# Loading one block's inputs early, spreading its query projection over the other block's attention, and moving a final projection

## The chip, the cores and the metric

One core of a Trainium2 chip runs the whole program. The metric is the device time of one execution in microseconds. The engines are TensorE (PE: matmuls; PEld: its weight loads), VectorE (DVE), ScalarE (ACT), GpSimd (POOL) and SyncE (SP), which here issues every transfer.

## The reference

Two independent attention blocks on inputs of 2048 tokens and 640 channels, with 32 heads of 20 channels, in bfloat16. Their results stand side by side in the output, A in columns 0 to 639 and B in columns 640 to 1279.

```python
# A: four segments of 512 tokens; inside a segment causal attention, beside it a
#    memory M, z of all earlier segments
logits = einsum('bhqd,bhkd->bhqk', qs, ks) * scale + mask
a_dot = einsum('bhqk,bhkd->bhqd', softmax(logits), vs)
pq = phi(qs)                       # phi(t) = t + 1 if t > 0 else exp(t)
a_mem = einsum('bhld,bhde->bhle', pq, M) / (einsum('bhld,bhd->bhl', pq, z) + 1e-6)
o = g * a_mem + (1 - g) * a_dot    # g = sigmoid(beta), per head
M = M + einsum('bhld,bhle->bhde', phi(ks), vs);  z = z + sum(phi(ks))
out_A = concat(o) @ A_wo
# B: causal attention in a window of 256 tokens
q, k, v = split(B_x @ B_wqkv)
scores = where(0 <= i - j < 256, q @ k.T * scale, -1e9)
out_B = (softmax(scores) @ v) @ B_wo
```

## The kernel before

Tokens come in 16 tiles of 128, heads in 8 groups of four; a head of 20 channels is padded to 32 partitions. The program is written stage after stage with tile pools; a scheduler puts each engine's instructions in one fixed order, mostly that of the text, and an engine runs its own in that order. A tile of a pool that takes the memory of a released pool waits for the last users of that memory.

The stages in order of time:

1. **B's projections.** `load_w` fetches wo_A and wo_B, `load_xT` fetches B's input transposed (xT_B, five transposing transfers), then comes the weight wallB. `proj_qk_compact_to_dram` makes the keys (kcB) and the queries (qcB), 20 steps of five 512-column matmuls each, and stores each result in one transfer to DRAM (kcdB, qcdB). `proj_v` makes the values in 16 tiles, five matmuls of 512 columns and five of 128 each; VectorE evicts them into vaug_B. PSUM has two buffers for either kind.
2. **A's keys and values.** The pool p2 opens when stage 1's pool closes. Into it go xT_A (five transposing transfers), wraw_k, wv_A and wraw_q. VectorE scales wv_A with a row made from beta, and copies wraw_k and wraw_q into zeroed padded weights (wk_pad, wq_pad; GpSimd zeroes them). `proj_qk_padded_to_dram` makes the padded keys in 32 steps of five 512-column matmuls, eight steps to a 1 MB store of stp0 or stp1 to kdA; `proj_v` makes the values, two tiles to a store of vstA0 or vstA1 to vdA.
3. **B's attention** (`attention_B`): for each head group g, 16 iterations kt over key tiles. An iteration makes scores of four heads (L298, up to 384 query columns), ScalarE turns them into probabilities pt (L305, two instructions, at most 768 elements wide), VectorE masks the diagonal (L307), GpSimd the far edge (L313). Every second iteration multiplies pt with the values (L341, 16 matmuls of 128 or 256 columns), and `normalize_block` transposes and divides (L226 to L244) into o_tok_B. The two PSUM buffers psS hold the scores. The keys and queries of a group are fetched into kg0, kg1, qg0 and qg1 in turn, zero-filled once from zt. At the end of each iteration `next(aux_gen)` traces one step of A's query projection: 32 steps like those of the keys (PSUM ppa, evicted into stp0 and stp1), and after every eighth a store to qdA.
4. **B's final projection** (`final_projection`): for each token tile five transposes, an eviction, five matmuls of 512 columns and five of 128, an eviction, and the store.
5. **A's segments** (`segment_A`): four times, for 512 tokens: k_s, v_s and q_s are fetched from kdA, vdA and qdA; for each head group the feature maps (ek, eq, pkt, pq), scores (L429), ScalarE's exponentials (L437), GpSimd's mask (L443), the value matmuls (L462), the memory products (L406, L473); at the segment's end the final projection of its own four tiles.

Of the kernel before, what the change touches and what calls it, by code (L numbers as in the profile page):

```python
# [8 lines left out]
ALU = mybir.AluOpType  # L9
# [3 lines left out]
P = 128  # L13
# [9 lines left out]
class _K:  # L23
# [250 lines left out]
    def attention_B(self, wk, psum, qcd, kcd, vaug, o_tok, aux_gen=None):  # L274
# [8 lines left out]
        for g in range(G):  # L283
# [6 lines left out]
            for kt in range(T):  # L290
# [62 lines left out]
                if aux_gen is not None:  # L353
                    next(aux_gen, None)
# [140 lines left out]
    def run(self, A_x, A_wq, A_wk, A_wv, A_wo, A_beta, B_x, B_wqkv, B_wo, out2d):  # L495
# [8 lines left out]
        with tc.tile_pool(name="pers", bufs=1) as pers:  # L504
            wo_A = self.load_w(pers, "wo_A", A_wo)
            wo_B = self.load_w(pers, "wo_B", B_wo)
            with tc.tile_pool(name="ob", bufs=1) as pob:
                o_tok_B = pob.tile([P, T, D], BF16, name="o_tok_B")
                vaug_B = self.make_vaug_sbuf(pob, "vaug_B")
                pp1 = self.ctx_psum1 = tc.alloc_tile_pool(name="ps1pool", bufs=1,  # L510
                                                          space=bass.MemoryType.PSUM)
                self.build_consts(A_beta, pp1)

                def get_ps_1():
                    return pp1.tile([P, 512], F32, name="pps1", bufs=2)

                def get_ps2_1():
                    return pp1.tile([P, 2, 512], F32, name="pps2", bufs=2)
                with tc.tile_pool(name="p1b", bufs=1) as p1:
                    xT_B = self.load_xT(p1, B_x[0], "xT_B")  # L520
                    wall = self.load_w(p1, "wallB", B_wqkv)
                    qcB = p1.tile([P, MC, S], BF16, name="qcB")
                    kcB = p1.tile([P, MC, S], BF16, name="kcB")

                    def vsink_b(tt, flat):
                        nc.vector.tensor_copy(
                            out=vaug_B[:, tt, :, 0:DH],
                            in_=flat[:, 0:D].rearrange("p (h e) -> p h e", e=DH))
                    for _ in self.proj_qk_compact_to_dram(wall[:, :, D:2 * D], xT_B,
                                                          kcB, kcdB, get_ps_1):  # L530
                        pass
                    for _ in self.proj_qk_compact_to_dram(wall[:, :, 0:D], xT_B, qcB,
                                                          qcdB, get_ps_1):
                        pass
                    for _ in self.proj_v(wall[:, :, 2 * D:3 * D], xT_B, get_ps2_1,
                                         vsink_b):
                        pass
                p2 = tc.alloc_tile_pool(name="p2", bufs=1)
# [4 lines left out]
                nc.vector.tensor_tensor(  # L543
                    out=wv_A[:], in0=wv_A[:],
                    in1=self.omh640[:].unsqueeze(1).to_broadcast([P, KT, D]),
                    op=ALU.mult)
                wk_pad = self.pad_weight(p2, "wk_padA", wraw_k[:])
                wq_pad = self.pad_weight(p2, "wq_padA", wraw_q[:])
                stps = [p2.tile([P, G, 512], BF16, name="stp0"),
                        p2.tile([P, G, 512], BF16, name="stp1")]  # L550
                vsts = [self.make_vst(p2, "vstA0", 2), self.make_vst(p2, "vstA1", 2)]

                def vsink_a(tt, flat):
# [12 lines left out]
                with tc.tile_pool(name="ps2pool", bufs=1, space=bass.MemoryType.PSUM) as pp2:  # L566
# [11 lines left out]
                    for _ in agen:  # L578
                        pass
# [76 lines left out]
```

## Time and profile before

| | us |
|---|---|
| median of four runs | 838.94 (837.62 to 842.25) |
| the profiled execution | 837.62 |
| its span | 835.9 |
| TensorE matmuls busy | 716.3 (86% of the span) |
| VectorE busy | 416.9 (50%) |
| ScalarE busy | 374.5 (45%) |
| GpSimd busy | 242.5 (29%) |

The busy shares are averages over stages that have different limits. The page's slices give the TensorE clock that was granted in each fortieth of the span; in the rows below it stands behind the busy times, and there 1.00 is 2.4 GHz and 0.50 is 1.2 GHz. The same instruction counts as busy for longer at the lower clock, so a busy share has to be read beside the clock.

### The profile page before, as it was taken

The page shows a single profiled execution, that of the slowest core. Times are in us where ns is not written, and L with a number is a line of the kernel's source. Part 1 is how long each engine was busy: PE and PEld are TensorE (multiplying, and loading weights), DVE is VectorE, ACT ScalarE, POOL GpSimd, SP SyncE. Part 2 cuts the span into 40 slices and gives each one's busy share as a digit, 9 for nine tenths or more (in the row PEclk, how much of TensorE's full clock was granted, in tenths as well). Part 3 has the DMA queues.
Part 4 walks back from the last instruction along what each step waited for, and adds up shares of the span by engine and source line. Part 5 has one row for each costly group of instructions (what it writes and reads, how often), then busy time and mean ns, then how long its engine had stood idle before and what let it go on. Part 6 is the DMA issues. An engine that isn't in the chain of part 4 may idle for free.

```text
span 835.9 us, 12231 instructions
## 1 busy us (share of the span) xinstructions
PE 716.3 (86%) x4768; PEld 308.3 (37%) x4768; DVE 416.9 (50%) x1013; ACT 374.5 (45%) x498; POOL 242.5 (29%) x498
## 2 busy tenths in 40 slices
PE   2799559999999999999998828887998898988996
PEld 1345324444444333333334413334333433342333
DVE  5366356566666544444444533235455745463343
ACT  0000000045658767666672017663666366526651
POOL 9000410023334424333341004331433134313431
PEclk9999869999999755555556975557555755565557
DMA  9434553421212100101000263005000500000000
GB/s 224 135 136 148 111 164 122 180 102 51 83 66 68 32 27 7 32 1 33 1 1 16 79 224 110 1 1 183 1 2 1 182 1 1 1 24 9 1 0 32
DMA packets 54028, 54.26 MB, mean 65 GB/s; under 512 B 22802, under 2 KB 46482, under 8 KB 53970
## 3 DMA queue, kind: packets, MB, share of 16 engines
q1 hardware_dynamic: 53970, 53.49, 20.4%
q8 instruction: 37, 0.61, 0.3%
q14 instruction: 21, 0.17, 0.1%
HBM read 24.38 MB, written 23.07 MB: 57 GB/s over the span
## 4 chain that ended last, share of the span: by engine, by line
PE 60%; DVE 10%; ACT 9%; POOL 7%; issue 6%; DMA 4%; SPq 4%; DVEq 0%; ACTq 0%
PE psO L341 11%; PE ps L462 9%; POOL pt L443 7%; PE psS L298 6%; ACT pt L437 6%; PE pps L147 5%; DVE oc L226 5%; PE pps L181 4%; PE ps L429 4%; PE pps L197 4%; SPq L119 3%; PE ppa L181 3%; PE ps L262 3%; PE fps L262 2%; ACT pt L305 2%
## 5 line engine op out<-in xcount | busy, mean ns | idle before, releaser
L305 ACT ACTIVATE pt<-psS 128x768 bf16<-128x768 f32 (+2 forms) x256 | 185.6, 770 | 253.8 <-PE psS L298 208.2
L437 ACT ACTIVATE pt<-ps 128x1024 bf16<-128x1024 f32 (+1 forms) x192 | 161.7, 881 | 96.2 <-PE ps L429 86.2
L443 POOL TENSOR_SCALAR_AFFINE_SELECT pt<-pt 128x256 bf16<-128x256 bf16 x256 | 105.8, 432 | 229.6 <-ACT pt L437 226.5
L313 POOL TENSOR_SCALAR_AFFINE_SELECT pt<-pt 128x256 bf16<-128x256 bf16 x224 | 103.7, 463 | 233.7 <-ACT pt L305 233.7
L462 PE MATMUL ps<-pt,v_s 128*32 128x128 bf16 (+3 forms) x512 | 117.4, 455 | 11.0 <-POOL pt L443 7.5
L341 PE MATMUL psO<-pt,vaug_B 128*32 128x256 bf16 (+1 forms) x960 | 126.0, 316 | 0.4
L298 PE MATMUL psS<-qg,kg 32*128 32x384 bf16 (+2 forms) x512 | 100.6, 414 | 6.6 <-ACT pt L305 5.3
L307 DVE TENSOR_TENSOR pt<-pt,cmask 128x256 bf16<-128x256 bf16 x256 | 79.8, 312 | 52.0 <-ACT pt L305 50.4
L429 PE MATMUL ps<-q_s,k_s 32*128 32x128 bf16 (+3 forms) x512 | 93.6, 433 | 11.8 <-ACT pt L437 7.8
L226 DVE CAST oc<-ps 128x512 bf16<-128x512 f32 x56 | 38.5, 688 | 95.2 <-PE ps L462 93.1
L341 PEld LDWEIGHTS <-vaug_B 128*32 128x32 bf16 x960 | 59.7, 110 | 68.9 <-issue 57.4
L462 PEld LDWEIGHTS <-v_s 128*32 128x32 bf16 x512 | 39.7, 119 | 75.6 <-issue 73.3
L226 DVE CAST oc<-psO 128x256 bf16<-128x256 f32 x64 | 27.1, 423 | 60.6 <-PE psO L341 60.5
L181 PE MATMUL pps<-xT_A,wk_padA 128*128 128x512 bf16 x160 | 36.8, 394 | 17.9 <-DVE wk_padA L133 17.9
L228 PEld LDWEIGHTS <-oc 128*128 128x128 bf16 x352 | 27.9, 120 | 61.3 <-DVE oc L226 60.8
L147 PE MATMUL pps<-xT_B,wallB 128*128 128x512 bf16 x200 | 45.1, 390 | 5.3 <-DMA wallB<-in_B_wqkv_dram 5.3
L379 ACT ACTIVATE ek<-k_s 128x512 bf16<-128x512 bf16 x24 | 14.9, 624 | 74.0 <-DMA k_s<-kdA 46.9
L429 PEld LDWEIGHTS <-k_s 32*128 32x128 bf16 x512 | 20.7, 100 | 73.5 <-issue 72.5
L181 PE MATMUL ppa<-xT_A,wq_padA 128*128 128x512 bf16 x160 | 44.7, 380 | 3.0 <-DVE stp L184 2.4
L298 PEld LDWEIGHTS <-kg 32*128 32x128 bf16 x512 | 25.0, 96 | 58.3 <-issue 50.5
L228 PE MATMUL ps<-ident,oc 128*128 128x128 bf16 x224 | 33.3, 302 | 14.4 <-DVE oc L226 14.4
L147 PEld LDWEIGHTS <-wallB 128*128 128x128 bf16 x200 | 19.9, 100 | 30.1 <-DMA wallB<-in_B_wqkv_dram 5.4
(97 smaller groups left out, 684.5 us busy)
## 6 DMA issues: line engine op xcount, KB each, us to landing
out_dram<-otile SPq DMA_DIRECT2D x32, 160.0 KB
kdA<-stp SPq DMA_DIRECT2D x4, 1024.0 KB
vdA<-vstA SPq DMA_DIRECT2D x8, 512.0 KB
qdA<-stp SPq DMA_DIRECT2D x4, 1024.0 KB
k_s<-kdA SPq DMA_DIRECT2D x4, 1024.0 KB
v_s<-vdA SPq DMA_DIRECT2D x4, 1024.0 KB
q_s<-qdA SPq DMA_DIRECT2D x4, 1024.0 KB
kcdB<-kcB SPq DMA_DIRECT2D x1, 2560.0 KB
```

Source lines behind the costliest of these rows:

```text
L147: nc.tensor.matmul(ps[:, 0:512], lhsT=w_ap[:, kt, m * P:(m + 1) * P], rhs=xT[:, kt, cs], start=(kt == 0), stop=(kt == KT - 1))
L181: nc.tensor.matmul(ps[:, 0:512], lhsT=wpad[:, kt, g * P:(g + 1) * P], rhs=xT[:, kt, cs], start=(kt == 0), stop=(kt == KT - 1))
L226: nc.vector.tensor_copy(out=oc[:, 0:ncols], in_=num_ps[:, 0:ncols])
L298: nc.tensor.matmul(pss[hp][:, i, 0:N], lhsT=kg[rows, kt * P:(kt + 1) * P], rhs=qg[rows, kt * P:kt * P + N], start=True, stop=True, tile_po ...
L305: nc.scalar.activation(out=pt[:, :, 0:N], in_=pss[hp][:, :, 0:N], func=ACT.Exp, scale=scale)
L307: nc.vector.tensor_tensor(out=pt[:, :, 0:P], in0=pt[:, :, 0:P], in1=self.cmask[:].unsqueeze(1).to_broadcast([P, 2, P]), op=ALU.mult)
L313: nc.gpsimd.affine_select(out=blk, in_=blk, pattern=[[0, 2], [-1, P]], compare_op=ALU.is_ge, fill=0.0, base=-1, channel_multiplier=1)
L341: nc.tensor.matmul(O[orows, oc0:oc0 + ncol], lhsT=vg[:, k2, q4, 0:HD], rhs=pts[(hp, k2)][:, i, rc0:rc0 + ncol], start=(n_ == 0), stop=(n_ ...
L429: nc.tensor.matmul(pss[hp][:, i, coloff[kt]:coloff[kt] + n], lhsT=k_s[rows, g, q0:q0 + P], rhs=q_s[rows, g, q0:q0 + n], start=True, stop=True,
L437: nc.scalar.activation(out=pt[:, :, 0:used], in_=pss[hp][:, :, 0:used], func=ACT.Exp, scale=scale)
L443: nc.gpsimd.affine_select(out=blk, in_=blk, pattern=[[0, 2], [1, P]], compare_op=ALU.is_ge, fill=0.0, base=0, channel_multiplier=-1)
L462: nc.tensor.matmul(NUM[orows, P * kt:P * kt + n], lhsT=v_s[:, kt, h, 0:HD], rhs=pt[:, i, co:co + n], start=(cnt == 1), stop=(cnt == nmm), ...
```

## The change

Four things are changed, in `run` and in the last line of `attention_B`'s loop. The pool a_in for xT_A, wraw_k, wv_A, wraw_q and wk_pad is opened before stage 1, and their transfers are issued right behind that of wallB. The scaling of wv_A and the copy into wk_pad stay on VectorE, with a dependency that keeps them behind the eviction of B's ninth value tile. The query projection's generator is advanced in three of ten iterations in place of each. And stage 4 is gone: o_tok_B stays allocated, and behind each of A's segments four of B's tiles are projected, in the PSUM buffers of the segments (ps1, ps2).

```diff
-                if aux_gen is not None:
+                if aux_gen is not None and (g * T + kt) * 3 % 10 < 3:
                     next(aux_gen, None)
...
+            pain = tc.alloc_tile_pool(name="a_in", bufs=1)
+            xT_A = pain.tile([P, KT, S], BF16, name="xT_A")
+            wraw_k = pain.tile([P, KT, D], BF16, name="wraw_k")
+            wv_A = pain.tile([P, KT, D], BF16, name="wv_A")
+            wraw_q = pain.tile([P, KT, D], BF16, name="wraw_q")
+            wk_pad = pain.tile([P, KT, G * P], BF16, name="wk_padA")
...
+            nc.gpsimd.memset(wk_pad[:], 0.0)
...
+                xT_B = self.load_xT(p1, B_x[0], "xT_B")
+                wall = self.load_w(p1, "wallB", B_wqkv)
+                x2dA = A_x[0]
+                for kt in range(KT):
+                    nc.sync.dma_start_transpose(out=xT_A[:, kt, :],
+                                                in_=x2dA[:, kt * P:(kt + 1) * P])
+                nc.sync.dma_start(out=wraw_k[:],
+                                  in_=A_wk.rearrange("(kt p) n -> p kt n", p=P))
...
+                def vsink_b(tt, flat):
+                    self.vcast = nc.vector.tensor_copy(
+                        out=vaug_B[:, tt, :, 0:DH],
                         in_=flat[:, 0:D].rearrange("p (h e) -> p h e", e=DH))
+                    if tt == 8:
+                        self.vcast0 = self.vcast
...
+            p2 = tc.alloc_tile_pool(name="p2", bufs=1)
-                xT_A = self.load_xT(p2, A_x[0], "xT_A")
-                wraw_k = self.load_w(p2, "wraw_k", A_wk)
-                wv_A = self.load_w(p2, "wv_A", A_wv)
-                wraw_q = self.load_w(p2, "wraw_q", A_wq)
+            sc = nc.vector.tensor_tensor(
+                out=wv_A[:], in0=wv_A[:],
+                in1=self.omh640[:].unsqueeze(1).to_broadcast([P, KT, D]),
+                op=ALU.mult)
+            tc.add_manual_dep(sc.ins, self.vcast0.ins.name, mybir.DependencyInfo(mybir.DependencyClass.NoSync, mybir.DependencyReason.DATA),
...
-                with tc.tile_pool(name="finB", bufs=1) as finB, \
-                        tc.tile_pool(name="ps3pool", bufs=1, space=bass.MemoryType.PSUM) as pp3:
-                    self.final_projection(finB, pp3, o_tok_B, wo_B, out2d, D, range(T))
...
+                        btts = range(seg * nbt, min(T, (seg + 1) * nbt))
+                        self.final_projection(finA, pp4, o_tok_B, wo_B, out2d, D, btts,
+                                              tag2="ps2", bufs2=2, tag1="ps1",
+                                              bufs1=3)
```

The order moves at three places that matter below. The first is SP's queue at the start. Before, the zero-fills of the attention's buffers (qg, kg) stand behind wallB:

```order
L126 DMA wallB<-in_B_wqkv_dram 128x5x1920
L169 DMA qg_1102<-zt 12x2048 x4
L169 DMA qg_1103<-zt 12x2048 x4
L169 DMA kg_1104<-zt 12x2048 x4
L169 DMA kg_1105<-zt 12x2048 x4
L152 DMA kcdB<-kcB 128x5x2048
```

Now A's inputs stand there, and the zero-fills come behind the stores of kcdB and qcdB:

```order
L126 DMA wallB<-in_B_wqkv_dram 128x5x1920
L530 DMA_TRANSPOSE xT_A<-in_A_x_dram 128x2048 x5
L532 DMA wraw_k<-in_A_wk_dram 128x5x640
L534 DMA wv_A<-in_A_wv_dram 128x5x640
L536 DMA wraw_q<-in_A_wq_dram 128x5x640
L152 DMA kcdB<-kcB 128x5x2048
L152 DMA qcdB<-qcB 128x5x2048
L169 DMA qg_1105<-zt 12x2048 x4
```

The transposing transfers and the three weights moved from behind the last of stage 1's loads to directly behind wallB.

The second place is TensorE at the start of a head group. Before, at the start of group 3 (psO_2555 is the output of group 2's last pair of tiles, kg1_1105 the next group's keys), the first score of the new group stands behind eleven of the sixteen value matmuls:

```order
L341 MATMUL psO_2555<-pt_2540,vaug_B_76 32x256
L341 LDWEIGHTS vaug_B_76
L341 MATMUL psO_2555<-pt_2488,vaug_B_76 32x128
L298 LDWEIGHTS kg1_1105
L298 MATMUL psS_2590<-qg1_1103,kg1_1105 128x384
L341 LDWEIGHTS vaug_B_76
L341 MATMUL psO_2555<-pt_2552,vaug_B_76 32x128
```

Now, at the start of group 1 (and in the same way at those of groups 2 to 6), all four first scores stand behind the third value matmul, and a matmul of the query projection (ppa) follows them:

```order
L298 LDWEIGHTS kg1_1108
L298 MATMUL psS_1586<-qg1_1106,kg1_1108 128x384
L181 LDWEIGHTS wq_padA_658
L181 MATMUL ppa_1101<-xT_A_82,wq_padA_658 128x512
L341 LDWEIGHTS vaug_B_76
L341 MATMUL psO_1550<-pt_1544,vaug_B_76 32x128
```

The projection's matmuls, which before ended in group 2, now stand there in six of the seven group starts; the start of group 7 reads as that of group 3 before.

The third place is SP's queue between the attention and A's segments. Now the loads of the first two segments stand behind the last store of the query projection, where before the sixteen stores of B's final projection stood ahead of them:

```order
L161 DMA qg_1106<-qcdB 20x2048 x4
L186 DMA qdA<-stp_662 128x8x512
L615 DMA k_s<-kdA 128x8x512
L618 DMA v_s<-vdA 128x4x1024
L621 DMA q_s<-qdA 128x8x512
```

The stores of both final projections moved behind the loads of the first two segments.

## Rows read from the trace of the kernel before

**Rows 1.** Stages: window, length, busy time and count of each engine, PEclk, DMA, GB/s.
```profile
174.50:277.00 102.50, 95.57 (x747) 42.80 (x746) 64.51 (x196) 68.08 (x96) 40.87 (x84) 1.00 0.19 60
277.00:449.50 172.50, 163.87 (x1017) 63.07 (x1015) 78.33 (x284) 117.55 (x160) 62.84 (x140) 0.51 0.06 16
449.50:486.60 37.10, 30.10 (x242) 17.81 (x240) 20.25 (x34) 0.00 (x0) 0.95 (x1) 0.92 0.18 67
500.00:835.90 335.90, 292.83 (x2044) 117.19 (x2043) 155.11 (x365) 184.30 (x235) 105.79 (x256) 0.56 0.11 36
```

**Rows 2.** Instructions on the tile ppa: durations min/median/max in ns, first and last start.
```profile
L181 PE MATMUL ppa<-xT_A,wq_padA x160: 376/379/390, 174.7 to 257.9; 128*128 128x512 bf16 x160
```

**Rows 3.** ScalarE's timeline, 258 to 284 us: start, length, instruction [idle before it].
```profile
264.87 2.92 ACT L305 ACTIVATE pt<-psS 128x768 bf16<-128x768 f32 x4 [0.21 <-PE psS L298]
268.00 2.92 ACT L305 ACTIVATE pt<-psS 128x768 bf16<-128x768 f32 x4 [0.21 <-PE psS L298]
...
274.26 1.82 ACT L305 ACTIVATE pt<-psS 128x768 bf16<-128x768 f32 x3 [0.21 <-PE psS L298]
276.23 0.66 ACT L305 ACTIVATE pt<-psS 128x256 bf16<-128x256 f32 x2 [0.15 <-PE psS L298]
278.55 5.31 ACT L305 ACTIVATE pt<-psS 128x768 bf16<-128x768 f32 x7 [1.66 <-issue]
```

**Rows 4.** The chain that ended last: start, length, what.
```profile
17.66 10.66 DMA wallB<-in_B_wqkv_dram
...
119.58 32.38 PE pps L181 x150
...
188.23 1.21 issue
193.25 1.26 issue
...
310.13 2.62 issue
344.49 2.62 issue
```

**Rows 5.** Single microseconds at the start of group 3, columns as in rows 1.
```profile
280.00:281.00 1.00, 0.53 (x5) 0.20 (x4) 0.50 (x2) 1.00 (x3) 0.69 (x2) 1.00 0.75 160
281.00:282.00 1.00, 1.00 (x8) 0.29 (x6) 0.38 (x2) 1.00 (x2) 0.82 (x2) 0.55 0.18 33
```

**Rows 6.** Single microseconds: the start of group 1, and of A's second segment.
```profile
211.00:212.00 1.00, 0.56 (x5) 0.28 (x3) 1.00 (x4) 0.79 (x3) 0.00 (x0) 1.00 0.23 41
584.00:585.00 1.00, 0.58 (x3) 0.28 (x3) 0.00 (x0) 1.00 (x3) 0.75 (x2) 0.94 0.00 0
```

**Rows 7.** Timeline of all engines between stages 1 and 2.
```profile
95.42 11.35 SPq L119 DMA_TRANSPOSE xT_A<-in_A_x_dram  x5
...
112.20 0.99 DVE L133 COPY wk_padA<-wraw_k 128x3200 bf16<-128x3200 bf16 x1 [15.95 <-DMA wraw_k<-in_A_wk_dram]
...
113.25 4.29 PE L181 MATMUL pps<-xT_A,wk_padA 128*128 128x512 bf16 x10 [17.86 <-DVE wk_padA L133]
...
114.30 3.49 DVE L543 TENSOR_TENSOR wv_A<-wv_A,omh 128x3200 bf16<-128x3200 bf16 x1 [1.11 <-DMA wv_A<-in_A_wv_dram]
```

**Rows 8.** Timeline of all engines between stages 4 and 5.
```profile
489.98 0.49 SPq L603 DMA_DIRECT2D q_s<-qdA  x1
...
499.92 0.61 PE L429 MATMUL ps<-q_s,k_s 32*128 32x512 bf16 x4 [2.03 <-DMA q_s<-qdA]
```

**Rows 9.** Groups by form: line, engine, shapes, count | busy, mean ns | idle before, releaser.
```profile
L526 DVE CAST vaug_B<-pps 128x640 bf16<-128x640 f32 x16 | 13.2, 824 | 8.9 <-PE pps L201 8.8
```

**Rows 10.** TensorE's timeline in B's final projection.
```profile
457.58 1.25 PE L262 MATMUL fps<-wo_B,oTc 128*128 128x512 bf16 x5 [0.76 <-DVE oTc L259]
...
458.95 1.24 PE L262 MATMUL fps<-wo_B,oTc 128*128 128x512 bf16 x5
...
461.79 1.25 PE L262 MATMUL fps<-wo_B,oTc 128*128 128x512 bf16 x5 [0.76 <-DVE oTc L259]
```

More of the change, by code (lines that the diff above doesn't have):

```diff
@@ L503, in run @@
         kcdB = self.dram.tile([MC, P, S], BF16, name="kcdB")
-        with tc.tile_pool(name="pers", bufs=1) as pers:
+        with tc.tile_pool(name="pers", bufs=1) as pers, \
+                tc.tile_pool(name="ob", bufs=1) as pob:
             wo_A = self.load_w(pers, "wo_A", A_wo)
             wo_B = self.load_w(pers, "wo_B", B_wo)
[L507 to L538, printed above, removed]
-                xT_A = self.load_xT(p2, A_x[0], "xT_A")
-                wraw_k = self.load_w(p2, "wraw_k", A_wk)
-                wv_A = self.load_w(p2, "wv_A", A_wv)
-                wraw_q = self.load_w(p2, "wraw_q", A_wq)
[L543 to L553, printed above, removed]
-                    vst = vsts[(tt // 2) % 2]
-                    nc.vector.tensor_copy(
-                        out=vst[:, tt % 2, :, 0:DH],
@@ L566, in run @@
-                with tc.tile_pool(name="ps2pool", bufs=1, space=bass.MemoryType.PSUM) as pp2:
-                    pa = [pp2.tile([P, 2, 512], F32, name="ppa", bufs=1)]
-                    tog = [0]
-                    def get_ps_a():
-                        tog[0] ^= 1
-                        return pa[0][:, tog[0], :]
-                    agen = self.proj_qk_padded_to_dram(wq_pad, xT_A, stps, qdA,
-                                                       get_ps_a)
-                    with tc.tile_pool(name="wkB", bufs=1) as wkB:
-                        self.attention_B(wkB, pp2, qcdB, kcdB, vaug_B, o_tok_B,
-                                         aux_gen=agen)
-                    for _ in agen:
-                        pass
@@ new lines, in run, with get_ps_a @@
+            for _ in self.proj_qk_padded_to_dram(wk_pad, xT_A, stps, kdA, get_ps_1):
+                pass
+            for _ in self.proj_v(wv_A[:], xT_A, get_ps2_1, vsink_a):
+                pass
+            pp1.release()
+            with tc.tile_pool(name="ps2pool", bufs=1, space=bass.MemoryType.PSUM) as pp2:
+                pa = [pp2.tile([P, 2, 512], F32, name="ppa", bufs=1)]
+                tog = [0]
+                def get_ps_a():
+                    tog[0] ^= 1
+                    return pa[0][:, tog[0], :]
+                agen = self.proj_qk_padded_to_dram(wq_pad, xT_A, stps, qdA, get_ps_a)
+                with tc.tile_pool(name="wkB", bufs=1) as wkB:
+                    self.attention_B(wkB, pp2, qcdB, kcdB, vaug_B, o_tok_B,
+                                     aux_gen=agen)
+                for _ in agen:
+                    pass
@@ L584, in run @@
+            p2.release()
+            pain.release()
             with tc.tile_pool(name="oa", bufs=1) as poa, \
```

48 lines of the change are left out of this document (41 added, 7 removed).

## The prediction

> **What bounds the kernel now.** The page's slices show a granted TensorE clock that is full at first and half later; I cut the span into its stages to put times on that [rows 1]. The sliding-window attention of block B runs from 174.5 to 449.5 us, and TensorE is busy 93 to 95% of it in both of its parts; but the first 102.5 us ran at 1.00 of the clock (2.4 GHz) and the last 172.5 us at 0.51 (1.2 GHz). The first part also carries all 160 matmuls of the query projection of block A, the last of them at 257.9 us [rows 2]. So in attention the clock decides what is late. At the full clock ScalarE is the limit where no projection stands: from 264.87 to 268.00, a pair of iterations, its four exponentials take 2.92 of 3.13 us [rows 3]. At half clock TensorE is: the head groups of 16 iterations begin 344.49 - 310.13 = **34.4 us** apart [rows 4].
>
> The price of one group at the full clock, with no projection beside it, comes from the ScalarE timeline. A group has 28 wide exponentials and four short ones. From 274.26 to 278.55 us stand one wide, the four short ones and the gap to the next group, 4.29 us; the other 27 wide ones at 3.13 / 4 take 21.1 [rows 3]. Together **25.4 us**, 9 less than at half clock. The first part held three groups and the projection: (102.5 - 3 x 25.4) / 32 = **0.82 us for each of the 32 projection steps** at the full clock.
>
> When does the clock fall? The projection ends at 258.3, and the clock stays full for 23 us more on attention alone. It falls at 281.5, at the start of group 3: ScalarE had waited 1.66 us for that group's first scores [rows 3], then TensorE was busy 0.53 of the microsecond before the fall [rows 5]. At the start of group 1 projection matmuls stood in the gap, and the clock stayed at 1.00 although one microsecond was busy only 0.56 (the first row of [rows 6]).
>
> The other two idle places are the fronts of the stages. From 95.4 to 117.8 us TensorE waits for the inputs of block A: the five transposing loads take 11.35 us of SP's queue, wraw_k ends a 15.95 us wait of VectorE, wv_A is scaled in 3.49 us, ending at 117.8 [rows 7]. And from 449.5 to 499.92 there is B's final projection (37.1 us [rows 1]) and then a wait for q_s, whose issue stands on SP behind the final projection's stores [rows 8].
>
> **The change, term 1: A's inputs are loaded during B's projections.** The 22.4 us between 95.4 and 117.8 go. Ten matmuls of the key projection ran in that hole, in 4.29 us at half clock [rows 7]; at the full clock 150 took 32.38 us, 0.216 each [rows 4], so 2.2 us come back. The scaling (3.49 us) and the copy into wk_pad (0.99 us) now stand on VectorE between the evictions of B's value projection (after the ninth and the eleventh, by the order). An eviction takes 0.82 us [rows 9] of the 1.37 that the ten matmuls of such a tile take (458.95 - 457.58, the same shape [rows 10]), and two PSUM buffers cover about one tile: 3.49 + 2 x 0.82 - 2 x 1.37 = 2.4 us of TensorE stall. The copy into wq_pad waits for a GpSimd memset that can start only after B's last read; three key evictions stand ahead of it, and I give it 0.7 us. On SP the eight transfers pass the store of kcdB and the zero-fills; the zero-fills now wait for B's weights to be released and stand ahead of the first kdA store, which is due only 8 steps (8.6 us) later. Behind them the first group's keys and queries alternate with the vdA stores, the last query row behind the sixth of eight, so about 5 us before attention needs it. Sum: -22.4 + 2.2 + 2.4 + 0.7 = **-17**, between -20 (stalls absorbed) and -6 (next sentence). The unknown here is wallB, which landed 10.66 us after its issue with only the zero-fills behind it [rows 4]; now the five transposes are issued right behind it. If they took nothing from it, 0; if all their 11.35 us came first, +11.4. I take 0, the end that the row is nearer to: 2.4 MB landed in 10.66 us with sixteen transfers issued behind them. The Trainium skill, page "DMA: Bandwidth & Descriptors", section "Queues, rings and completion order", says that each engine consumes the descriptors of a ring in order; by that the cost is 0 as well, and no run so far shows it for this pair.
>
> **Term 2: the projection steps are spread over attention.** A step is traced in three of ten iterations. By the order the 32 steps now stand from iteration 1 to 99 of 128, about 3.2 iterations apart, and at the starts of groups 1 to 6 projection matmuls stand among the first scores; the start of group 7 has none and reads as group 3 did before. I take the clock as full through groups 0 to 6 and lost in group 7: the trace had 23 us of plain attention without loss inside a group, and lost the clock only where a group start had nothing to fill it. The order also puts all four first scores of the next group ahead of most value matmuls, so ScalarE waits less there. Then 7 x 25.4 + 32 x 0.82 + 34.4 = 238.4 us in place of 449.5 - 174.5 = 275.0: **-37**. With two steps a pair of iterations took 193.25 - 188.23 = 5.02 us [rows 4], so TensorE's own part is 5.02 - 2 x 1.08 = 2.86; one step in 1.6 pairs then costs at least 1.6 x 2.86 + 1.08 - 1.6 x 3.13 = 0.65 us, and at most its own 5 x 0.216 = 1.08. So -42 to -28, and 9 us more if group 7 keeps the clock as well.
>
> **Term 3: B's final projection moves behind A's segments.** Between the end of attention (449.5 [rows 1]) and the first scores of A (499.92 [rows 8]) lie 50.4 us. Now k_s, v_s and q_s stand on SP behind the last qdA store, which waits for the 32nd projection step, some 28 iterations (over 40 us) before attention ends; what hides them is those iterations, and uncovered they cost the old 13 us. I leave 2 us for the first scores, keys and PSUM turnover. The 16 tiles come back, four behind each segment: at the full clock two tiles took 461.79 - 457.58 = 4.21 us [rows 10]. The order batches transposes by three tiles, not two, and the first three tiles of a burst are A's, which pay the warm-up as before. 16 x 2.0 = 32 us, between 16 x 1.85 (1.37 for the matmuls, half a us for five transposes) and 16 x 2.3. -50.4 + 2 + 32 = **-16**, between -19 and 0 (the loads uncovered). A's segments run at 0.56 now [rows 1] and I expect no other clock: before, the clock came back inside each final projection and was lost again at the thin start of the next segment, on a busy share of 0.58 (the second row of [rows 6]); that start is the same.
>
> **Sum.** The profiled execution took 837.62 us, 1.7 more than its span; it is the fastest of four, whose median is 838.94. 837.6 - 17 - 36.6 - 16.4 = **767.6 us**.
>
> **Rivals.** *The clock falls early and does not return (slower).* If a burst of five 512-column matmuls every 3.2 iterations is not enough at some group start, TensorE-bound groups follow that carry the projection at half clock: 34.4 + 4.57 x 5 x 0.43 = 44.2 us in place of 25.4 + 4.57 x 0.82 = 29.2, so 15 us a group. Lost at the start of group 1: six groups, 767.6 + 90 = 858. Lost at group 2: 843. From there it is slower than before. For it: the clock fell on a busy share of 0.53 [rows 5], and attention at half clock never regained it although TensorE was 95% busy [rows 1]. Against it: the filled group start that kept it [rows 6]. If the first bursts already fail, group 0 pays too: 873. The Trainium skill, page "TensorE: Matmul & The Clock Gate", section "HAM oscillation — how this bites in real kernels", tells of a kernel whose short dense bursts, split by waits, were throttled in every pass of the loop, and advises to keep dense work together; that speaks against spreading it, and gives the 873. The 23 us in which plain attention kept the clock speak against that rule here.
>
> *It falls later, or falls and returns.* Lost from group 6: 783; from group 3: 828; each loss with a return within the group costs 5 to 10 (a third to two thirds of the 15).
>
> *The prefetch collides.* wallB shares its transfer with the transposes: +11.4, 779; with the seam loads uncovered as well, 792.
>
> **How the numbers follow.** The forecast as summed, with or without group 7's clock: 0.66 (748 to 790; the low end is 767.6 - 9 for group 7 - 5 for the steps - 3 - 3 for the ends of terms 1 and 3). Later fall or falls with return: 0.19. Early fall: 0.09, of which 0.08 is slower by over 0.5%. Collision: 0.06. The range 748 to 805 leaves out the early fall and the worse half of the later falls, about 0.19. Half a per cent is 4.2 us, about what a measurement here can tell from no change. Faster 0.90, same 0.02, slower 0.08.
>
> **What would show it.** In the profile after: TensorE never idle for over 3 us between 28 and the end of the key projection (term 1), and its first wallB matmul still at 28.4; granted clock 1.00 in each stretch of 10 us of attention up to about group 7 (term 2), and the groups about 29 us apart; the first scores of A within 3 us of attention's last transposes, and eight tiles behind each segment in some 16 to 18 us (term 3). A clock of 0.5 in attention before group 7 makes the prediction wrong by 15 us a group; a first matmul at 35 or later makes term 1 wrong.

## The result and the profile after

The changed kernel takes 765.05 us (median of 11 runs, 756.55 to 768.06), the kernel before 839.92 us (16 runs); the ratio is 0.908, with a 95% interval of 0.905 to 0.910. The forecast was 767.6. The profiled execution took 765.45 us, 1.7 of it outside its span of 763.7, so it is compared with the 837.62 of the profiled execution before.

The stages of the changed kernel answer to [rows 1] and have the same columns: window, length, busy time and count of PE, PEld, DVE, ACT and POOL, granted TensorE clock, DMA share, GB/s.

```profile
158.40:330.30 171.90, 170.15 (x1344) 77.06 (x1343) 108.32 (x364) 136.35 (x192) 80.28 (x168) 1.00 0.16 46
330.30:337.00 6.70, 6.20 (x45) 2.69 (x44) 3.87 (x14) 5.18 (x7) 3.80 (x7) 1.00 0.38 111
337.00:399.50 62.50, 59.67 (x374) 23.22 (x372) 28.35 (x104) 41.99 (x58) 22.47 (x51) 0.50 0.35 116
400.30:763.70 363.40, 320.53 (x2304) 134.39 (x2304) 180.00 (x406) 187.05 (x240) 106.52 (x256) 0.59 0.10 33
```

Attention starts at 158.4 in place of 174.5 (-16.1 us). It takes 241.1 us in place of 275.0 (-33.9): six groups at the full clock in 171.9 us, with TensorE busy for 170.15 of them, 6.7 us more of group 6 at it, then 62.5 us at half clock. A's first scores stand at 400.31 in place of 499.92. From there to the end it is 363.4 us in place of 335.9, because the 16 tiles of B's final projection are now inside (+27.5). With the 50.4 us that went at the seam, the sum is -16.1 - 33.9 - 49.6 + 27.5 = -72.1.

The seam on TensorE's timeline (start, length, instruction, idle before it and what ended it): the last transposes of attention, then A's first scores, 0.86 us later, where [rows 8] had a wait for q_s.

```profile
399.06 0.40 PE L228 MATMUL psO<-ident,oc 128*128 128x128 bf16 x2 [0.52 <-DVE oc L226]
400.31 0.62 PE L429 MATMUL ps<-q_s,k_s 32*128 32x512 bf16 x4 [0.86 <-DVE o_tok_B L244]
```

The front, from the chain of work that ended last: the first wallB matmuls start at 28.70 (28.36 on the chain before), and what they waited for is no longer wallB, as in [rows 4], but the column constants that VectorE makes (grow) and TensorE turns.

```profile
23.37 3.82 DVE grow L103
27.24 1.47 PE pps L107 x6
28.70 45.54 PE pps L147 x200
```

These constants come 5.7 us later than before (their copy into colv starts at 28.74, and did at 23.08), most of it because of the change itself: the zeroing of wk_pad now stands at the start of GpSimd's work, and VectorE's two copies into grow beside it take 3.95 us. Before, with no GpSimd instruction beside them, the same two took 0.34 (timeline of the changed kernel, then of the kernel before):

```profile
22.75 4.35 POOL L518 MEMSET wk_padA<- 128x5120 bf16 x1
23.30 3.95 DVE L103 COPY grow<-e 1x128 f32<-1x128 f32 x2
```

```profile
21.31 0.34 DVE L103 COPY grow<-e 1x128 f32<-1x128 f32 x2
```

And the place where [rows 7] had the 22.4 us, from the timeline: VectorE scales wv_A among B's value evictions, and TensorE waits once for it; the key projection runs on without a gap, and waits once more, for an eviction that stands behind the copy into wq_pad.

```profile
87.47 3.48 DVE L557 TENSOR_TENSOR wv_A<-wv_A,omh 128x3200 bf16<-128x3200 bf16 x1
91.74 1.24 PE L197 MATMUL pps<-wallB,xT_B 128*128 128x512 bf16 x5 [2.33 <-DVE vaug_B L542]
98.53 5.56 PE L181 MATMUL pps<-xT_A,wk_padA 128*128 128x512 bf16 x25
103.06 4.39 POOL L216 MEMSET vstA<- 128x2048 bf16 x2
103.16 2.56 DVE L133 COPY wq_padA<-wraw_q 128x3200 bf16<-128x3200 bf16 x1 [0.49 <-POOL wq_padA L132]
106.36 1.89 PE L181 MATMUL pps<-xT_A,wk_padA 128*128 128x512 bf16 x8 [1.62 <-DVE stp L184]
```

The clock is the first thing that does not fit the forecast. It was to fall at the start of group 7. ScalarE's timeline has group 6 starting at 330.33 and group 7 at 365.60; the last projection matmul starts at 334.53, and single microseconds (columns as in the stages) show the clock gone at 337, inside group 6:

```profile
330.33 1.51 ACT L305 ACTIVATE pt<-psS 128x768 bf16<-128x768 f32 x2 [0.31 <-issue]
365.60 5.46 ACT L305 ACTIVATE pt<-psS 128x768 bf16<-128x768 f32 x7 [2.62 <-issue]
```

```profile
335.00:336.00 1.00, 0.84 (x7) 0.30 (x6) 1.00 (x3) 0.69 (x2) 1.00 (x2) 1.00 0.00 0
336.00:337.00 1.00, 0.66 (x5) 0.40 (x6) 0.58 (x3) 1.00 (x2) 0.81 (x2) 1.00 0.37 132
337.00:338.00 1.00, 1.00 (x8) 0.35 (x8) 0.56 (x3) 1.00 (x3) 0.68 (x2) 0.52 0.98 347
```

Not every execution does this. Over the recorded executions the mean granted clock is 0.765 in those of 763.6 to 765.6 us, and 0.781 to 0.784 in the four of 756.6 to 759.7 us; 768.1 us has 0.762. The experiments below show both places of the fall.

### The profile page after: what moved, and what is told of

Its sections match the earlier page's. It is cut to its first block, busy times and chain, and to the rows that moved or that the text cites. A ratio compares the mean times of both kernels' runs of the same rounds, so it can differ in the third digit from the quotient of the medians.

```text
span 763.7 us, 12251 instructions
## 1 busy us (share of the span) xinstructions
PE 688.3 (90%) x4768; PEld 303.7 (40%) x4768; DVE 423.0 (55%) x1013; ACT 372.1 (49%) x498; POOL 248.9 (33%) x498
## 4 chain that ended last, share of the span: by engine, by line
PE 70%; DVE 8%; ACT 8%; POOL 8%; issue 3%; DMA 1%; SPq 0%; DVEq 0%; ACTq 0%; POOLq 0%
PE psO L341 11%; PE ps L462 10%; PE psS L298 10%; POOL pt L443 8%; ACT pt L437 7%; PE pps L147 6%; PE ppa L181 6%; PE ps L262 5%; PE ps L429 4%; PE pps L181 4%; PE pps L197 4%; DVE oc L226 3%; PE ps L228 2%; PE psO L228 2%; PE ps L406 2%
## 5 line engine op out<-in xcount | busy, mean ns | idle before, releaser
L305 ACT ACTIVATE pt<-psS 128x768 bf16<-128x768 f32 (+2 forms) x256 | 183.5, 770 | 205.6 <-PE psS L298 182.7
L443 POOL TENSOR_SCALAR_AFFINE_SELECT pt<-pt 128x256 bf16<-128x256 bf16 x256 | 106.5, 436 | 238.8 <-ACT pt L437 236.3
L313 POOL TENSOR_SCALAR_AFFINE_SELECT pt<-pt 128x256 bf16<-128x256 bf16 x224 | 105.7, 472 | 180.5 <-ACT pt L305 179.8
L341 PE MATMUL psO<-pt,vaug_B 128*32 128x256 bf16 (+1 forms) x960 | 105.3, 275 | 0.0
L298 PE MATMUL psS<-qg,kg 32*128 32x384 bf16 (+2 forms) x512 | 98.1, 354 | 2.7 <-ACT pt L305 1.0
L307 DVE TENSOR_TENSOR pt<-pt,cmask 128x256 bf16<-128x256 bf16 x256 | 78.1, 305 | 37.5 <-ACT pt L305 35.8
L341 PEld LDWEIGHTS <-vaug_B 128*32 128x32 bf16 x960 | 53.5, 101 | 47.9 <-issue 37.6
L181 PE MATMUL ppa<-xT_A,wq_padA 128*128 128x512 bf16 x160 | 58.4, 388 | 0.0
L298 PEld LDWEIGHTS <-kg 32*128 32x128 bf16 x512 | 27.8, 92 | 55.0 <-issue 43.1
L270 DVE CAST otile<-ps 128x640 bf16<-128x640 f32 x32 | 26.4, 824 | 23.6 <-PE ps L266 23.6
L181 PE MATMUL pps<-xT_A,wk_padA 128*128 128x512 bf16 x160 | 34.9, 379 | 1.6 <-DVE stp L184 1.6
```

The costliest lines, as they stand in the source:

```text
L181: nc.tensor.matmul(ps[:, 0:512], lhsT=wpad[:, kt, g * P:(g + 1) * P], rhs=xT[:, kt, cs], start=(kt == 0), stop=(kt == KT - 1))
L298: nc.tensor.matmul(pss[hp][:, i, 0:N], lhsT=kg[rows, kt * P:(kt + 1) * P], rhs=qg[rows, kt * P:kt * P + N], start=True, stop=True, tile_po ...
L305: nc.scalar.activation(out=pt[:, :, 0:N], in_=pss[hp][:, :, 0:N], func=ACT.Exp, scale=scale)
L313: nc.gpsimd.affine_select(out=blk, in_=blk, pattern=[[0, 2], [-1, P]], compare_op=ALU.is_ge, fill=0.0, base=-1, channel_multiplier=1)
L341: nc.tensor.matmul(O[orows, oc0:oc0 + ncol], lhsT=vg[:, k2, q4, 0:HD], rhs=pts[(hp, k2)][:, i, rc0:rc0 + ncol], start=(n_ == 0), stop=(n_ ...
L443: nc.gpsimd.affine_select(out=blk, in_=blk, pattern=[[0, 2], [1, P]], compare_op=ALU.is_ge, fill=0.0, base=0, channel_multiplier=-1)
```

## Experiments: what each part is worth

**The spreading alone, and all but the spreading.** In the kernel before, and undone in the changed kernel:

```diff
-                if aux_gen is not None:
+                if aux_gen is not None and (g * T + kt) * 3 % 10 < 3:
```

> The kernel before with one edit: the projection step is traced in three of ten iterations. Theory (spreading is worth what attention itself got shorter, 275.0 to about 241 us, because the clock stays up to group 6): 839.9 - 34 = 806, the front and the seam as before. Rival (part of that came from the earlier front or from the seam, for instance because qdA's last store now ends late and A's first loads wait for it): 815 to 840 with the loss visible between attention's end and A's first scores.

Measured: 804.78 us (797.64 to 805.28), ratio to before 0.955 (0.950 to 0.960), -35.0 us.

> The changed kernel with the projection step traced in each iteration again. Theory: the projection ends in group 2, the clock falls within 25 us behind it, at the start of group 3, and attention takes 275 in place of 241 us: 765 + 34 = 799. Rival (the clock's fall is set by time or by what ran before attention, not by the projection): 760 to 775, or a fall at another group than group 3.

Measured: 802.70 us (799.87 to 804.16), 37.7 more than the changed kernel; the clock falls at 269, with the last projection matmul at 243.1. Both numbers agree with term 2 as measured (33.9). The gain is attention's own and does not lean on the other parts.

**The early loads alone.** The changed kernel with the condition taken out and the final projection put back between attention and the segments; o_tok_B keeps its pool open to the end.

> The changed kernel with the spreading and the move both undone, so that only the early loads of A's inputs are left. Theory (the three parts add up; the front gave 174.5 - 158.4 = 16.1 us): 839.9 - 16 = 824. Rival (the parts lean on each other, the clock falling at another place since attention starts from another state): over 5 us from 824.

Measured: 807.85 us (804.50 to 807.92), ratio 0.961 (0.958 to 0.963): -32.0, twice the expected. Attention starts at 158.6 and takes its old 275 us; the other half is at the seam. This run differs from the kernel before in two things, the early loads and o_tok_B's pool, which stays open, so that the segments' tiles take over other memory. SP's timeline has the loads of A's first segment right behind the last store to qdA, at 249 us, 186 us ahead of B's final projection, and on TensorE (the second block) A's first scores follow the last tile at 470.58, where before 14 us lay between (485.71 to 499.92).

```profile
248.99 0.38 SPq L618 DMA_DIRECT2D k_s<-kdA  x1
250.04 0.50 SPq L624 DMA_DIRECT2D q_s<-qdA  x1
```

```profile
468.90 0.44 PE L266 MATMUL fps<-wo_B,oTc 128*128 128x128 bf16 x5
470.26 0.38 PE L389 MATMUL ps<-ident,pkt 128*128 128x128 bf16 x4 [0.92 <-DVE otile L270]
470.58 0.39 PE L429 MATMUL ps<-q_s,k_s 32*128 32x512 bf16 x4
```

So the wait for q_s did not need the move of the final projection. What released the loads is the memory they go into. That reading was argued from this run; a later one shows it. In fill_last (below) extra matmuls read xT_A and wq_pad until attention ends, whose memory the segments' tiles take over. There the same three loads go out at 428.79 in place of 340.29, although nothing but these matmuls was added, and TensorE waits for q_s again (SP's timeline, then TensorE's, then what SP waited for before it issued k_s: in the kernel before, in the changed kernel and in fill_last):

```profile
428.79 0.38 SPq L620 DMA_DIRECT2D k_s<-kdA  x1
429.84 0.50 SPq L626 DMA_DIRECT2D q_s<-qdA  x1
```

```profile
440.02 0.62 PE L433 MATMUL ps<-q_s,k_s 32*128 32x512 bf16 x4 [1.93 <-DMA q_s<-qdA]
```

```profile
SPq L597 <- DMA out_dram<-otile: 1.4, 1, 1.4
SPq L615 <- DMA qdA<-stp: 4.2, 1, 4.2
SPq L620 <- PE psO L348: 86.5, 1, 86.5
```

Each of the three waits for the last reader of tiles of a released pool: the final projection's output tiles before, the projection's stp now, and the extra matmuls (L348) in fill_last.

**All but the move.** The changed kernel without the calls behind the segments, and with this put back:

```diff
             p2.release()
             pain.release()
+            with tc.tile_pool(name="finB", bufs=1) as finB, \
+                    tc.tile_pool(name="ps3pool", bufs=1, space=bass.MemoryType.PSUM) as pp3:
+                self.final_projection(finB, pp3, o_tok_B, wo_B, out2d, D, range(T))
```

> The changed kernel with B's final projection back between attention and A's segments. Theory: the seam is 37 us of tiles and some us of waiting again, and 27.4 us of tiles behind the segments go: between 765 + 37 + 1 - 27 = 776 (q_s is loaded early) and 765 + 50.4 - 0.9 - 27.4 = 787 (its loads stand behind the final projection's stores as before). I take 787, since the stores are traced ahead of the loads. Rival (moving gains nothing, the tiles cost the same in either place): 765 to 770.

Measured: 771.97 us (763.45 to 775.27), ratio 0.916 (0.909 to 0.922). The move itself is worth about 7 us by the medians (9.8 between the profiled executions), not 22, and the intervals of the two kernels touch. The 16 tiles take 35.3 us between the stages (401.0 to 436.3, and 1.2 more to A's first scores) and 27.5 us behind the segments. The three parts add up: -35.0 - 32.0 - 6.9 = -73.9, measured -74.9.

## Experiments: what holds the clock

In the changed kernel the scheduler set the projection's 160 matmuls among attention's mostly one by one, from 159.2 to 334.5, one per 1.1 us. To put the steps at chosen iterations, the first matmul of a step was bound behind the last score matmul of the iteration in which it is traced:

```diff
-                    nc.tensor.matmul(ps[:, 0:512], lhsT=wpad[:, kt, g * P:(g + 1) * P],
+                    mm = nc.tensor.matmul(ps[:, 0:512], lhsT=wpad[:, kt, g * P:(g + 1) * P],
...
+                    self.pin(mm, kt)
...
-                        nc.tensor.matmul(pss[hp][:, i, 0:N],
+                        self.smm = nc.tensor.matmul(pss[hp][:, i, 0:N],
...
-                if aux_gen is not None and (g * T + kt) * 3 % 10 < 3:
+                if aux_gen is not None and kt in (3, 5, 7, 9, 11):
```

**No projection at the group starts** (inner_only, the diff above).

> The changed kernel with the steps bound to iterations 3, 5, 7, 9 and 11 of each group, 32 steps up to iteration 108, so that no projection matmul stands within three iterations of any group start. Theory 1 (an unfilled group start loses the clock): lost at the start of group 1, six groups that pay 15 us: 840 to 858. Theory 2 (projection work anywhere in the last 25 us keeps it): clock full until about group 7, 755 to 768.

Measured: 813.82 us (809.24 to 816.56), ratio 0.969 (0.965 to 0.974), between the theories. The clock falls at unfilled group starts, as theory 1 says: first at 163, in attention's first iterations and ahead of the first projection matmul at 165.4, then at 197 (group 1 begins at 195.00 on ScalarE). But it comes back, which neither theory had: five projection matmuls run from 201.10, three and two with eight value matmuls between them, and at 204 the clock is 1.00. Single microseconds and TensorE's timeline:

```profile
196.00:197.00 1.00, 0.79 (x5) 0.28 (x4) 0.66 (x3) 1.00 (x2) 0.82 (x2) 1.00 0.61 143
197.00:198.00 1.00, 0.74 (x6) 0.23 (x5) 0.35 (x2) 1.00 (x3) 0.64 (x3) 0.57 0.27 78
...
203.00:204.00 1.00, 1.00 (x7) 0.17 (x3) 0.00 (x0) 0.00 (x0) 0.00 (x0) 0.52 0.00 0
204.00:205.00 1.00, 0.90 (x10) 0.41 (x9) 0.78 (x2) 0.07 (x1) 0.00 (x0) 1.00 0.00 0
```

```profile
201.10 1.46 PE L181 MATMUL ppa<-xT_A,wq_padA 128*128 128x512 bf16 x3
203.24 0.94 PE L181 MATMUL ppa<-xT_A,wq_padA 128*128 128x512 bf16 x2
```

Through attention there are eleven such falls, the last for good at 412, and attention takes 287 us. Eight of them stand within 5 us of a group start; three (218, 286 and 354) stand inside a group, so theory 1 does not cover all. The Trainium skill, page "TensorE: Matmul & The Clock Gate", section "HAM oscillation — how this bites in real kernels", tells of a throttle in each pass of a loop whose short dense bursts are split by waits for transfers. Here the clock goes and comes in the same way, though between the bursts stand narrow matmuls and not such waits (TensorE is busy 0.74 and more in the microseconds above). The changed kernel's trace shows no such thing: there the scheduler placed the steps, and from 158.4 to 337 nothing falls.

**The steps reach further** (rate_9_32: bound as above).

```diff
-                if aux_gen is not None and (g * T + kt) * 3 % 10 < 3:
+                if aux_gen is not None and (g * T + kt) * 9 % 32 < 9:
```

> The changed kernel with nine steps in 32 iterations, each step's first matmul bound behind the scores of its own iteration, so that the 32 steps reach from iteration 1 to 122 of 128 and the last group has its share. Theory 1 (a group start without projection matmuls loses the clock) and theory 2 (it is lost within 25 us of the projection's end, wherever that is) both: full clock through group 7, attention about 8 x 25.4 + 32 x 0.8 = 229 in place of 241 us: 752, between 745 and 757. Rival (the clock falls after some 180 us of attention whatever runs): 765 or more.

Measured: 781.58 us (774.20 to 785.51), ratio 0.930 (0.925 to 0.936). Both theories missed: the clock falls five times between 250 and 342 although steps stand up to iteration 122, each time for 3 to 10 us, and falls for good at 394. Attention takes 245 us. Bound steps, bursts of five matmuls with two or three iterations between them here and up to seven in inner_only, hold the clock less well than the scheduler's mixture.

**Extra matmuls in the kernel before** (before_filler, bound as above).

```diff
-                    next(aux_gen, None)
+                    if next(aux_gen, 1) == 1 and (g * T + kt) * 3 % 10 < 3:
+                        self.filler()
```

> The kernel before with 28 extra steps of five 512-column matmuls, whose results nobody reads, in three of ten iterations behind the end of the projection, up to the last iteration: 140 matmuls more and nothing else. If the clock alone makes the gain of the spreading: five groups keep the full clock, 5 x (34.4 - 25.4) = 45 less, 28 x 0.8 = 22.4 more: 839.9 - 23 = 817. If work counts and the fillers do not hold the clock: 28 x 5 x 0.43 = 60 more, 900. If the clock is held only in part: between.

Measured: 828.50 us (825.89 to 834.20), ratio 0.988 (0.984 to 0.993). 140 more matmuls make the kernel 11.8 us faster by the medians (9.1 between the profiled executions): attention takes 268.3 in place of 275.0 us at a mean clock of 0.96 in place of 0.69 (from the two parts in [rows 1]). Half of the 23 us expected came. The clock fell seven times in attention, for 2 to 4 us each; whether that is the other half was not separated. Here no work was moved, only added, and attention is still 6.7 us shorter: a clock that is held pays by itself. That it is all of what the spreading gains is not shown by this run.

**Whole-array or narrow matmuls in the last two groups** (fill_last, fill_narrow). The projection uses 128 by 128 of TensorE's array, attention's own matmuls 32 rows or 32 columns.

```diff
+                            if g * T + kt >= 96:
+                                nc.tensor.matmul(O[:, 256:512], lhsT=self.fw[:, 0, 0:P],
+                                                 rhs=self.fx[:, 0, 0:256],
+                                                 start=True, stop=True)
```

In fill_narrow the same line has `O[0:HD, 256:512]`, `self.fw[0:HD, 0, 0:HD]` and `self.fx[0:HD, 0, 0:256]`.

> The changed kernel with 64 extra matmuls of 128x128 weights and 256 columns, four to each pair of iterations of the last two head groups (6 and 7), written to an unused half of the PSUM tile psO and read by nobody; everything else stands in the order of the changed kernel. Theory A (the clock needs matmuls on the whole array, as the projection's are, evenly among attention's narrow ones): clock 1.00 to the end of attention, groups 6 and 7 at about 26 to 28 us in place of 35.3 and 34.3, so 765 - 15 = 750. Theory B (what counts is that TensorE does not pause, whatever it runs): the same here. Theory C (the clock falls after some 180 us of attention anyway): 64 x 0.21 = 13 us more at half clock, 778.

Measured: 805.74 us (805.36 to 814.56), ratio 0.961 (0.955 to 0.967).

> As fill_last, in the same order and with the same 64 x 256 columns, but each extra matmul uses 32 rows and 32 columns of the array, as attention's own matmuls use 32 of one side. Theory A: TensorE is as busy as in fill_last, and the clock falls all the same, in group 6 or at the start of group 7: 765 to 778. Theory B: the clock is held as in fill_last, 750.

Measured: 812.06 us (811.22 to 814.28), ratio 0.967 (0.963 to 0.971). All theories failed on the time. The last two groups take 99 us in fill_last in place of 69; 64 x 0.21 explains 13 of the 30, and the other 17 stay unexplained. The loads came late, as shown above (+10). On the clock: in fill_narrow it falls at 335, out of microseconds in which TensorE was busy throughout and ahead of the last projection matmul (336.2), so theory B falls. In fill_last it falls at 353 and does not come back before attention's last microsecond (428), so single wide matmuls among narrow ones did not hold it, and theory A falls in this form. The changed kernel's projection matmuls, which held it, stand mostly one by one too, but have 512 columns and not 256, and come closer together (160 in 176 us, here 64 in 94); which of the two counts no run separates. Single microseconds, of fill_narrow and then of fill_last:

```profile
334.00:335.00 1.00, 1.00 (x8) 0.45 (x6) 0.00 (x0) 0.20 (x1) 0.08 (x1) 1.00 0.00 0
335.00:336.00 1.00, 1.00 (x5) 0.33 (x4) 0.08 (x1) 0.61 (x1) 0.32 (x1) 0.54 0.00 0
```

```profile
352.00:353.00 1.00, 0.64 (x7) 0.23 (x5) 0.73 (x4) 1.00 (x3) 0.53 (x2) 1.00 0.00 0
353.00:354.00 1.00, 1.00 (x5) 0.39 (x5) 0.54 (x2) 1.00 (x2) 0.82 (x2) 0.67 0.00 0
```

## Experiments: the clock in A's segments

**The tiles among the head groups** (tiles_in_A).

```diff
+            if (seg * G + g) * 7 % 8 < 7:
+                self.one_tile(fin, psum, out2d)
```

> The changed kernel with the tiles of both final projections taken out of the ends of the segments and put one by one behind the head groups of A, seven in eight groups: 16 tiles of B and 12 of A's earlier segments; the last four stay at the end. If spread 128-row matmuls hold the clock in A's segments as they do in attention: their 363 us at 0.59 shrink to between 363 x 0.59 + 40 of waits = 254 and 320, total 655 to 722. If not (a tile takes one of the two score buffers and ScalarE waits, and the clock stays at 0.5 throughout since the dense bursts are gone): 363 to 400, total 765 to 805.

Measured: 815.89 us (810.83 to 818.56), ratio 0.970 (0.966 to 0.975), worse than the rival's range. The clock comes back with each tile, for about 3 us, and is lost again: 0.63 on the mean of the segments, which take 416.5 us. A tile takes one of the two PSUM buffers that the scores use, and ScalarE's longest wait for scores grew from 1.9 to 8.4 us; but over the segments it waits 96 us for them, against 88 in the changed kernel, so this is not where the 53 us more went. Its wait for pkt, which VectorE makes, grew from 37 to 86 us; what delays pkt was not traced.

**Extra matmuls in A's segments** (fill_A).

```diff
+        def filler():
+            nc.tensor.matmul(dMf[:, 256:512], lhsT=self.ident[:],
+                             rhs=wo_sb[:, 0, 0:256], start=True, stop=True)
```

It is called behind each set of four score matmuls and behind the value matmuls of each head, eight times a head group.

> The changed kernel with 256 extra matmuls of 128x128 weights and 256 columns in A's segments, eight to a head group, four behind the scores and four among the value matmuls, written to an unused half of the tile psdM and read by nobody. Theory A: the clock is held for most of the segments, and their 363 us shrink to about 300 (the chain of a head group at half clock holds 1.25 + 1.19 us of value matmuls and as much of scores in 8.6; these halve), 700. Rival (the waits for ScalarE and GpSimd inside a head group, not the kind of matmul, keep the clock down): half clock as before and 256 x 0.21 = 55 us of extra work, of which what fits the waits is free: 770 to 820.

Measured: 711.54, 723.48, 731.40 and 739.02 us, with mean granted clocks of 0.945, 0.917, 0.897 and 0.889. A ratio is not given, since the four lie so far apart. All are below the changed kernel's fastest, 756.55, so this kernel beats both. In the profiled execution the segments take 318.8 us at 0.93 in place of 363.4 at 0.59. The feature maps of successive head groups start 7.85 us apart, in place of 9.44 in the changed kernel at half clock (ScalarE's timeline in the second segment, of fill_A and then of the changed kernel):

```profile
493.57 0.62 ACT L383 ACTIVATE ek<-k_s 128x512 bf16<-128x512 bf16 x1
501.42 0.62 ACT L383 ACTIVATE ek<-k_s 128x512 bf16<-128x512 bf16 x1
```

```profile
513.64 0.62 ACT L379 ACTIVATE ek<-k_s 128x512 bf16<-128x512 bf16 x1
523.08 0.62 ACT L379 ACTIVATE ek<-k_s 128x512 bf16<-128x512 bf16 x1
```

This run also shows attention once more, with TensorE's order unchanged up to A's first scores. Here the microsecond behind the projection's end is busy only 0.56 and the clock stays; it falls at 359, at the start of group 7, as the forecast had it (single microseconds, then ScalarE's first instruction of group 7):

```profile
335.00:336.00 1.00, 0.56 (x5) 0.23 (x4) 0.62 (x3) 0.80 (x2) 0.89 (x2) 1.00 0.00 0
...
358.00:359.00 1.00, 0.54 (x4) 0.19 (x4) 0.51 (x2) 1.00 (x3) 0.71 (x2) 1.00 0.67 207
359.00:360.00 1.00, 0.96 (x10) 0.43 (x9) 0.37 (x2) 1.00 (x2) 0.82 (x2) 0.78 0.10 32
```

```profile
356.53 5.25 ACT L305 ACTIVATE pt<-psS 128x768 bf16<-128x768 f32 x7 [1.66 <-issue]
```

**The same matmuls, one by one** (fill_A_even). Each is bound behind the matmul that it follows in the text; in fill_A the scheduler had put up to seven in a row.

```diff
-        def filler():
-            nc.tensor.matmul(dMf[:, 256:512], lhsT=self.ident[:],
-                             rhs=wo_sb[:, 0, 0:256], start=True, stop=True)
+        def filler(mm):
+            fm = nc.tensor.matmul(dMf[:, 256:512], lhsT=self.ident[:],
+                                  rhs=wo_sb[:, 0, 0:256], start=True, stop=True)
+            self.tc.add_manual_dep(
+                fm.ins, mm.ins.name,
...
```

> As fill_A, with each of the 256 extra matmuls bound behind the score or value matmul that it follows in the text, so that they stand one by one among them and not in bursts of up to seven. If it is the even mixture of whole-array matmuls that holds the clock in A's segments: the falls inside the first segment go and the executions lie closer together, 695 to 712 in all. If the amount alone counts: the 711 to 739 of fill_A again. If the binding costs more (an extra matmul waits with its neighbour and holds up the scores behind it): over 725 at a clock of 0.9 or more.

Measured: 792.34 us (782.19 to 796.09), ratio 0.945 (0.943 to 0.947). The third case, and worse: in the profiled execution the segments take 386 us at 0.87. The order alone costs 1.2 us a head group at nearly the full clock (503.43 to 512.45 between two feature maps, 9.02 in place of 7.85, at a mean clock of 0.96), and the clock now falls fifteen times in the 32 head groups, three times in fill_A. Bursts of wide matmuls, left where the scheduler found room, did better on both counts. Whether all of fill_A's gain is the clock, or some of it the order that came with the extra matmuls, was not separated.

## Why the prediction was right, point by point

The forecast was 767.6 and the profiled execution took 765.45, but part of this agreement is luck. Terms 1 and 2 gave 0.9 and 2.7 us less than forecast, term 3 gave 5.7 more. Inside term 2, too, two errors cancel in part.

**Term 1** was right: -16.1 for -17. The stall behind the scaling was 2.33 us (2.4), that behind the copy into wq_pad 1.62 (0.7), because the copy itself took 2.56 us in place of 0.99. wallB cost nothing; as the chain now ends on the constants, the trace does not show how much earlier wallB was there.

**Term 2** had the right mechanism and nearly the size: -33.9 for -37. A group with projection steps took (330.33 - 159.31) / 6 = 28.5 us (29.2 forecast). The step that failed is "lost at the start of group 7" as the only case. In the profiled execution the clock fell one group earlier, behind the last projection matmul, and group 6 cost 35.3 us (330.33 to 365.60) in place of the 26.8 that it takes in fill_A's execution (329.77 to 356.53). The cheaper groups before it, 0.7 us each, gave back half of this. The reason that the prediction gave, an unfilled group start, is shown by inner_only and by fill_A. That it is the only trigger is not so (changed kernel, fill_narrow), and with the same order of TensorE's instructions the clock fell at 337 in one execution and at 359 in another. Of the six traces with the changed kernel's attention, four (the changed kernel, spread_alone, no_move, tiles_in_A) lose it about 2 us behind the last projection matmul, and two (fill_A, fill_A_even) 25 us behind it, at group 7. Why one and not the other stays open. (The prediction read the fall before at 281.5; the clock of 0.55 in the microsecond from 281 puts it near 281.1, which changes none of its sums.)

**Term 3** was -22.1 for -16. The mis-sized price is the tile: 27.5 / 16 = 1.72 us in place of 2.0. The first burst, eight tiles, takes 17.9 us from the first transposes at 471.09 to the last matmul at 488.99; the four bursts together take 70.7 us, and were 43.3 with four tiles each. The clock in the segments is 0.59 (0.56 before), up only through the longer bursts. And its reason was half wrong. The prediction held the queue, SP's sixteen stores, to be what kept A's loads late, and so put the seam's 14 us of waiting down to the move. By front_alone they were not the move's: the loads go early with the final projection in its old place. The rule that a tile waits for the last users of the memory it takes over stands in the section on the kernel before; the prediction did not ask whose memory k_s and q_s take. The move's own part is about 7 us.

**The rivals.** The early fall did not come with the scheduler's placing; bound steps make it real, with returns, at (813.8 - 765) / 11 = 4.4 us a fall on the mean, the bound order's own cost included, just under the 5 to 10 that the prediction gave for a loss with a return. The later fall (783 from group 6) happened as a place and not as a price: the half clock costs a group without projection 8.5 us, not the 15 of one that carries it. The prefetch did not collide.

## What to carry to other kernels

Work that one engine has to spare can be worth more as a means to hold its clock than as work off the path: look for the stretch at half clock, and for dense work that can stand in it; but let it fill gaps, and don't bind it to fixed places or put it into buffers that the stretch needs. A load that waits though its queue is free may be waiting for memory: look whose last reader must finish before its tile exists. And test a change of three parts part by part, since the sum can be right where a part's reason is not.

## What the runs showed of the hardware

A clock that was lost came back where five 512-column whole-array matmuls or the matmuls of a tile ran nearly in a row (inner_only: from 201.10, back at 204; tiles_in_A: from 433.72, back by 436), and not in 62.5 us of narrow matmuls with TensorE 95% busy (the changed kernel, 337 to 399.5). How much of the array a matmul uses seems to count beside how busy TensorE reads; no run changed that alone with the clock held.

VectorE and GpSimd held each other up. The copy into wq_pad took 2.56 us beside two memsets of vstA that took 4.39; before, apart from each other, it took 0.99, as did the copy of [rows 7], and the two memsets 3.55, 1.8 each. The copies into grow at the front, shown with the result, are a second case: they took 3.95 us beside the memset of wk_pad and ended at 27.25, 0.15 behind it; before they took 0.34. The Trainium skill, page "SBUF — State Buffer", section "SBUF: two separate sides", says that certain VectorE instructions and GpSimd's exclude each other for a whole instruction. By that the copy would wait for the first memset and end at 103.06 + 1.8 + 0.99 = 105.85 (an estimate from these rows); it ended at 105.72, so the trace agrees within 0.13 us.
